# VectorE's exponential as five fp16 bit patterns that TensorE sums in PV, on three of sixteen key blocks per unit instead of two

## The chip, the cores and the metric

The kernel runs on one core of a Trainium2 chip. The metric is device microseconds of one execution, median of three. A core has TensorE (PE, matrix multiplication into PSUM), ScalarE (ACT, here the exponential), VectorE (DVE), GpSimd (POOL), SyncE (SP, which issues DMAs), and 16 DMA engines. Each engine runs its own instructions in the order in which they were written, and waits on semaphores for the others.

## What is computed

Two attention problems of sequence length 2048, width 512 and 32 heads of 16 channels are computed, and their outputs stand side by side. Problem A works in four segments of 512 tokens: causal attention inside a segment, mixed by a gate with a linear-attention memory of the earlier segments. Problem B is plain full attention over 2048 keys. Cut to what matters here:

```python
def _B_ref(x, wqkv, wo):
    q, k, v = split_heads(x @ wqkv)                  # (B, H, S, 16) each
    scores = jnp.einsum('bhqd,bhkd->bhqk', q, k) * Dh ** (-0.5)
    p = _softmax(scores, axis=-1)
    o = jnp.einsum('bhqk,bhkd->bhqd', p, v)
    return merge_heads(o) @ wo

# A, per segment s: o = g * (phi(q) M) / (phi(q) z + 1e-6) + (1 - g) * causal_softmax(q k^T) v
return jnp.concatenate([a, b], axis=-1)
```

The work that dominates is the exponential of B's scores: 32 heads by 2048 queries by 2048 keys.

## The kernel before, in words

**Units.** The work is cut into 64 units, 32 of A and 32 of B. A unit is a chunk of 512 queries (`ch`), a group of eight heads (`rt`, 0 to 3) and one half of that group (`e`), so four heads `j`. The `order` list (L369 to L375) takes A's first segment, and then B's pairs of units (`e` 0 and 1) in turn with A's pairs of the later segments, until A's are used up; the last chunk of B has none between.

**Banks and tiles.** The scores of one key block (128 keys) for one head and 512 queries fill one PSUM bank, 128 x 512 in fp32. A unit of B has 16 key blocks of 4 banks, 64 in all; a pair of A units has 20. The banks that ScalarE is to exponentiate are put in a row and closed into tiles of alternately 3 and 2 banks (`BANKS`, L44; `close`, L415). For each tile `t` the loop at L757 writes, in this order: chores that are due (`run_until`), the score matmuls of the tile into `s_ps` and ScalarE's exponential of it into `pT` in bf16 (`scores`, L646, L655), the PV matmuls of up to two key blocks whose exponentials are at least two tiles old (`pv`, L730, called with `t - LAG`), some chores (projections, memory updates, outputs), filler matmuls (`idle_work`, L571), one score matmul for VectorE (`vscores`, L676), and as much VectorE work as its time credit allows (`vfill`, L632).

**PE's shapes.** Score matmuls contract over 32 rows, and the four heads use four row groups of the array. PV matmuls have 32 output columns, and the four heads use four column groups; a key block's four PV matmuls make one group of four. Projections use the whole array. All go through the helper `mm` (L77), so the profile gives them line L80 and they are told apart by their tiles. `mm` also counts an assumed cost in `work`. `idle_work` compares it with 74% of the tile's time (`PESHARE`) and issues matmuls of a zero matrix into the running accumulator (`acc<-zeros`) when PE has less to do than that.

**VectorE's exponential before.** For every B unit but the first, key blocks 0 and 1 (`VQUADS = 2`) are left out of ScalarE's tiles. Their scores go through a PSUM bank called `v_ps`. `vscores` scales and shifts each bank into 16-bit integers (L689, tile `vx`, four of them to a key block), so that the integer read as fp16 is a first estimate of the exponential. The generator `vexp` (L593) then corrects it by a polynomial: three tensor_scalar operations (L596) and three tensor_tensor operations (L599) on 128 x 2048 elements, in tiles `vf`, `vv` and `vx`. The result enters `pvq` as one more key block for PV. These blocks are planned over the span of the unit ahead of their own (L399, L424 to L444), so they are there when their unit begins.

**What holds things back.** `pvq` is sorted by unit, and `pv` works on one unit at a time, `cur`. PSUM has eight banks: five for the two score tiles, three under the tag `misc` (L335), which the unit's accumulator `acc`, `v_ps` and the PSUM of every projection share. When a unit's last PV matmul is written, `unit_done` (L694) has VectorE transpose the accumulator out and normalise it in pieces (`vfin`). The exponentials `pT` have six tiles in all (`PBUFS`).

**The check on sums.** `sums_ok` (L304) looks at all softmax denominators against `SUMS` (L35); out of bounds, a slow exact version would run at the end.

Of the kernel before, what the change touches and what calls it, by code (L numbers as in the profile page):

```python
# [34 lines left out]
SUMS = {"a": (2.0 ** -8, 2.0 ** 31), "b": (2.0 ** 7, 2.0 ** 15.5)}  # L35
XSCALE = SCALE * 1.4426950408889634 * 1024

C0, C1, C3 = 0.4580543, 0.4656991, 0.0762947
# [3 lines left out]
VWAIT = 3  # L42
VQUADS = 2
# [6 lines left out]
def kernel(  # L50
# [87 lines left out]
    def load_w(pool, name):  # L138

        t = pool.tile([P, 4, 3 * D], BF16, name=f"w_{name}", tag=f"w_{name}")  # L140
        srcs = ([B_wqkv[:, i * D:(i + 1) * D] for i in range(3)] if name == "b" else [A_wq, A_wk, A_wv])

        def load(eng, i, lo=0, hi=D):
            eng.dma_start(out=t[:, :, i * D + lo:i * D + hi],
                          in_=srcs[i][:, lo:hi].rearrange("(cc p) n -> p cc n", p=P))
        return t, load
# [20 lines left out]
    def do_k(mp, w, xT, rt, dst):  # L167
        ps = mp.tile([P, W], F32, name="k_ps", tag="misc")
        for cc in range(4):
            mm(ps[:], w[:, cc, D + rt * P:D + (rt + 1) * P], xT[:, cc, :], start=(cc == 0), stop=(cc == 3))  # L170
            if cc == 3:
                vlater(0.69, lambda: pin(nc.vector.tensor_copy(dst, ps[:])))
            yield

    def do_q(mp, wk, w, xT, rt, dst, phi=None):

        ps = mp.tile([P, W], F32, name="q_ps", tag="misc")
        for cc in range(4):
            mm(ps[:], w[:, cc, rt * P:(rt + 1) * P], xT[:, cc, :], start=(cc == 0), stop=(cc == 3))
# [22 lines left out]
    def do_v(mp, w, xT, kb, dst):  # L202
        ps = mp.tile([P, W], F32, name="v_ps", tag="misc")
        for cc in range(4):
            mm(ps[:], xT[:, cc, kb * P:(kb + 1) * P], w[:, cc, 2 * D:3 * D], start=(cc == 0), stop=(cc == 3))
# [124 lines left out]
    with ExitStack() as ms:  # L330
# [6 lines left out]
        wA, ld = load_w(big, "a")  # L337
# [8 lines left out]
        wB, ld = load_w(big, "b")  # L346
# [32 lines left out]
        for name, ch, rt in order:  # L379
# [4 lines left out]
            if name == "a":  # L384
# [7 lines left out]
                spans.append([(name, ch, rt), banks, []])  # L392
            else:

                for u in us:
                    quads_left[u["id"]] = S // P
                    nv = VQUADS if nb else 0
                    if nb:
                        spans[-1][2].extend((u, kb) for kb in range(nv))  # L399
                    spans.append([(name, ch, rt) if u is u0 else None,  # L400
                                  [(j, [(u, kb, 0, 512, 0)]) for kb in range(nv, S // P) for j in q4], []])
                    nb += 1

        for i in range(1, len(spans)):
            key = spans[i][0]
            if key and key[0] == "a" and spans[i][2]:
                spans[i - 1][1] += spans[i][1]
                spans[i - 1][2] += spans[i][2]
                spans[i - 1].append((key, len(spans[i - 1][1]) - len(spans[i][1])))
                spans[i] = None  # L410
        first_tile, tiles = {}, []
        vq = deque()
        act = deque()

        def close(n, v=None):  # L415
            tiles.append(([act.popleft() for _ in range(n)], v))
        for sp in spans:
            if sp is None:
                continue
            starts = {0: sp[0]} if sp[0] else {}  # L420
            for key, at in sp[3:]:
                starts[at] = key
            for u, kb in sp[2]:
                vq.append((u, kb, set(q4)))  # L424
            nv, na, placed = sum(len(left) for *_, left in vq), len(sp[1]), 0
            for i, bank in enumerate(sp[1]):
                if i in starts:
                    first_tile[starts[i]] = len(tiles)
                act.append(bank)
                n = BANKS[len(tiles) % 2]  # L430
                if len(act) < n:
                    continue
                v = None
                if vq and placed < nv and (placed + 0.5) * na <= nv * (i + 1):
                    js = vq[0][2] - {j for j, _ in act}
                    if js:
                        j = min(js)
                        u, kb, left = vq[0]
                        left.discard(j)
                        if not left:  # L440
                            vq.popleft()
                        first_tile.setdefault(("v", u["ch"], u["rt"]), len(tiles))
                        v = (j, (u, kb, 0, 512, 0))
                        placed += 1  # L444
                close(n, v)
        assert not vq
        while act:
            close(min(BANKS[len(tiles) % 2], len(act)))
# [70 lines left out]
        def b_kv_chores():  # L519
            v_ones(VB, S // P)  # L520
            for rt in range(NRT):
                for ch in range(4):
                    d = first_tile[("b", 0, rt)] + 5 * ch
                    chore(min(d, first_tile.get(("v", 0, rt), NT)) if ch == 0 else d,
                          do_k(mp, wB, xTB[ch], rt, KB[:, rt, ch * W:(ch + 1) * W]))
            for sb in range(S // P):
                chore(first_tile[("b", 0, 0)] + 4 + 4 * sb // 3,
                      do_v(mp, wB, xTB[sb // 4], sb % 4, v_heads(VB, sb)[:, :, 0:DH]))


        vfin, vwork, credit = deque(), deque(), [0.0]
# [46 lines left out]
        pvq = []  # L578
# [12 lines left out]
        vx, live = {}, [0]  # L591

        def vexp(q, xq):  # L593

            def ts(o, i, s1, s2, op0, op1):
                pin(nc.vector.tensor_scalar(o, i, s1, s2, op0, op1))  # L596

            def tt(o, i0, i1, op):
                pin(nc.vector.tensor_tensor(o, i0, i1, op=op))  # L599
            yield 0.69  # L600
            assert live[0] < 3
            live[0] += 1
            f = wk.tile([P, 4, 512], F16, name="vf", tag="vf")
            v = wk.tile([P, 4, 512], F16, name="vv", tag="vv")
# [7 lines left out]
            yield 0.69  # L612
# [3 lines left out]
            pd = xq[:].bitcast(F16)  # L616
            u, kb = q
            pvq.append(dict(u=u, kb=kb, t=now[0], v=True, parts=[(pd, j, j, (u, kb, 0, 512, 0)) for j in q4]))
            pvq.sort(key=lambda q: q["u"]["id"])
# [12 lines left out]
        def vfill(us):  # L632
            credit[0] = min(credit[0] + us, 1.4)
            while vfin or vwork:
                wq = vfin or vwork
                if wq is vwork and live[0] == 3 and not wq[0][2]:
# [9 lines left out]
        def scores(t):  # L646
            banks, vb = tiles[t]
# [17 lines left out]
            for sl, (j, segs) in enumerate(banks):  # L665
                for seg in segs:
# [5 lines left out]
                    q["parts"].append((pT, sl, j, seg))  # L672
                    q["t"] = t
            pvq.sort(key=lambda q: q["u"]["id"])

        def vscores(t):  # L676

            vb = tiles[t][1]
            if vb is None:
                return  # L680
            vt = mp.tile([P, 512], F32, name="v_ps", tag="misc")
            score(vt[:], vb[0], vb[1], True)
            u, kb = vb[1][0:2]
            if (u["id"], kb) not in vx:
                while len(vwork) >= VWAIT:
                    vpiece(vwork)
                vx[u["id"], kb] = [wk.tile([P, 4, 512], U16, name="vx", tag="vx", bufs=VWAIT + 2), 0]
            x = vx[u["id"], kb]
            pin(nc.vector.tensor_scalar(x[0][:, vb[0], :], vt[:], XSCALE, 15360.0, ALU.mult, ALU.add))  # L689
            x[1] += 1  # L690
            if x[1] == 4:
                vpush(vwork, vexp((u, kb), x[0]))
# [37 lines left out]
        def pv(t, lim):  # L730
# [7 lines left out]
            for q in ready[0:lim]:  # L738
                pvq.remove(q)
                live[0] -= "v" in q  # L740
# [6 lines left out]
                for pT, sl, j, (_, kb, col, w, c0) in q["parts"]:  # L747
# [9 lines left out]
        for t in range(NT):  # L757
# [13 lines left out]
            idle_work(0.1 + 0.427 * len(tiles[t][0]))  # L771
            flush()
            vscores(t)
            vfill((0.08 + 0.427 * len(tiles[t][0])) * VSHARE - (0.69 if tiles[t][1] else 0.0))
# [5 lines left out]
        vdrain(vwork)  # L780
# [41 lines left out]
    def exact_problem(name):  # L822
        is_a = name == "a"
        with ExitStack() as es:
# [17 lines left out]
            w, ld = load_w(big, name)  # L842
# [119 lines left out]
```

## Time and profile before

| quantity | value |
|---|---|
| median of three runs | 1050.23 us |
| the three runs | 1049.83, 1050.23, 1059.84 us |
| span of the profiled execution, first to last instruction | 1055.6 us |
| own time of the profiled execution | taken as 1059.84 us, the only one of the three longer than the span |
| mean granted TensorE clock | 0.976 of full |
| ScalarE busy | 984.7 us |
| TensorE busy | 967.6 us |
| VectorE busy | 759.8 us |
| GpSimd busy | 169.9 us |

How to read it: the span starts at the first and ends at the last instruction, and the own time holds what lies around it too (4.2 us here). Busy is the time in which at least one instruction of an engine was running. Matmuls overlap one another, so their mean duration is longer than the distance from one to the next; the same holds for ScalarE's exponentials. A row of the groups gives busy time, the mean ns of one instruction, and the idle time of the engine just before them with the instruction that ended it. The waits list who stood idle for whom. The chain follows the work that ended last back to the start.

### The profile page before, as it was taken

The page shows a single profiled execution, that of the slowest core. Times are in us where ns is not written, and L with a number is a line of the kernel's source. Part 1 is how long each engine was busy: PE and PEld are TensorE (multiplying, and loading weights), DVE is VectorE, ACT ScalarE, POOL GpSimd, SP SyncE. Part 2 cuts the span into 40 slices and gives each one's busy share as a digit, 9 for nine tenths or more (in the row PEclk, how much of TensorE's full clock was granted, in tenths as well). Part 3 has the DMA queues.
Part 4 walks back from the last instruction along what each step waited for, and adds up shares of the span by engine and source line. Part 5 has one row for each costly group of instructions (what it writes and reads, how often), then busy time and mean ns, then how long its engine had stood idle before and what let it go on. Part 6 is the DMA issues. An engine that isn't in the chain of part 4 may idle for free.

```text
span 1055.6 us, 17191 instructions
## 1 busy us (share of the span) xinstructions
PE 967.6 (92%) x6822; PEld 277.2 (26%) x6822; DVE 759.8 (72%) x1108; ACT 984.7 (93%) x877; POOL 169.9 (16%) x335
## 2 busy tenths in 40 slices
PE   8899999998999989999998999999999999999996
PEld 2222222222222222222222222222222222222221
DVE  2668787866888677788876788858576787776654
ACT  3799999998999989999999899999999999999995
POOL 3721210403013030030302204021020300000000
PEclk8999999998999989999999899999999999999998
DMA  8400000001000000010000000000000000000000
GB/s 179 100 7 21 6 2 6 1 2 25 6 1 13 29 7 6 2 25 6 2 6 1 21 26 1 7 1 1 2 1 1 2 30 11 1 1 2 1 1 25
DMA packets 35642, 15.36 MB, mean 15 GB/s; under 512 B 27360, under 2 KB 35552, under 8 KB 35552
## 3 DMA queue, kind: packets, MB, share of 16 engines
q1 hardware_dynamic: 33776, 13.78, 5.5%
q8 instruction: 55, 0.90, 0.4%
q10 hardware_dynamic: 1776, 0.40, 0.2%
q14 instruction: 35, 0.29, 0.1%
HBM read 4.20 MB, written 4.19 MB: 8 GB/s over the span
## 4 chain that ended last, share of the span: by engine, by line
ACT 40%; PE 31%; issue 12%; DVE 11%; POOL 3%; DMA 1%; SPq 0%; ACTq 0%; DVEq 0%; POOLq 0%
ACT pT L655 39%; PE acc L80 14%; PE s_ps L80 8%; PE v_ps L80 5%; DVE vv L599 2%; DVE vx L689 2%; POOL pT L663 2%; PE q_ps L80 1%; PE k_ps L80 1%; DVE vx L599 1%; PE o_ps L80 1%; DVE vv L596 1%; ACT ex L194 1%; DVE vf L596 1%; DVE tT L253 1%
## 5 line engine op out<-in xcount | busy, mean ns | idle before, releaser
L655 ACT ACTIVATE pT<-s_ps 128x1536 bf16<-128x1536 f32 x848 | 973.5, 1314 | 57.7 <-PE s_ps L80 53.0
L80 PE MATMUL s_ps<-qB,KB 32*128 32x512 bf16 x1800 | 310.8, 384 | 35.0 <-ACT pT L655 30.5
L80 PE MATMUL acc<-zeros 128*128 128x512 bf16 x1053 | 321.6, 390 | 0.0
L689 DVE TENSOR_SCALAR vx<-v_ps 128x512 uint16<-128x512 f32 x248 | 169.1, 683 | 122.2 <-PE v_ps L80 65.7
L80 PEld LDWEIGHTS <-KB 32*128 32x128 bf16 x2048 | 99.6, 91 | 339.6 <-issue 326.7
L663 POOL TENSOR_SCALAR_AFFINE_SELECT pT<-pT 128x256 bf16<-128x256 bf16 (+2 forms) x242 | 111.0, 487 | 322.7 <-ACT pT L655 322.1
L80 PE MATMUL acc<-pT,VB 128*32 128x512 bf16 x1800 | 144.4, 385 | 1.2 <-DVE tT L253 1.2
L80 PEld LDWEIGHTS <-zeros 128*128 128x128 bf16 x1069 | 84.6, 99 | 147.2 <-issue 111.7
L253 DVE STREAM_TRANSPOSE tT<-acc 128x512 f32<-128x512 f32 x64 | 45.7, 714 | 94.1 <-PE acc L80 93.9
L80 PE MATMUL v_ps<-qB,KB 32*128 32x512 bf16 x248 | 95.5, 385 | 9.2 <-DVE aT L260 3.4
L596 DVE TENSOR_SCALAR vv<-vv 128x2048 f16<-128x2048 f16 x124 | 86.7, 699 | 2.2
L599 DVE TENSOR_TENSOR vv<-vf 128x2048 f16<-128x2048 f16 x62 | 76.2, 1229 | 1.9
L599 DVE TENSOR_TENSOR vx<-vx,vv 128x2048 int16<-128x2048 uint16 x62 | 76.0, 1226 | 1.2
L599 DVE TENSOR_TENSOR vv<-vv,vf 128x2048 f16<-128x2048 f16 x62 | 76.0, 1227 | 1.1
L80 PE MATMUL s_ps<-qA,kA 32*128 32x384 bf16 (+3 forms) x512 | 56.8, 313 | 9.9 <-ACT pT L655 7.8
L186 POOL TENSOR_SCALAR qB<-qc,par 128x512 bf16<-128x512 bf16 x32 | 26.0, 823 | 232.1 <-DVE qc L183 229.2
L80 PEld LDWEIGHTS <-VB 128*32 128x32 bf16 x2048 | 32.4, 94 | 73.9 <-issue 73.8
L596 DVE TENSOR_SCALAR vf<-vx 128x2048 uint16<-128x2048 uint16 x62 | 43.3, 699 | 1.5
L186 POOL TENSOR_SCALAR qA<-qc,par 128x512 bf16<-128x512 bf16 x32 | 25.7, 815 | 114.9 <-DVE qc L183 114.8
L80 PE MATMUL acc<-pT,vA 128*32 128x128 bf16 (+3 forms) x512 | 39.0, 332 | 5.6 <-POOL pT L663 3.2
L80 PEld LDWEIGHTS <-kA 32*128 32x128 bf16 x512 | 17.8, 92 | 63.1 <-issue 61.2
L80 PE MATMUL acc<-vx,VB 128*32 128x512 f16 x248 | 24.7, 386 | 4.6 <-DVE vx L599 3.9
(88 smaller groups left out, 510.8 us busy)
## 6 DMA issues: line engine op xcount, KB each, us to landing
out_dram<-osb SPq DMA_DIRECT2D x31, 128.0 KB, 1.7
w_b<-in_B_wqkv_dram SPq DMA_DIRECT2D x3, 512.0 KB, 6.0
phk<-phkT SPq DMA_TRANSPOSE x48, 2.3
w_a<-in_A_wv_dram SPq DMA_DIRECT2D x1, 512.0 KB, 7.0
wo_a<-in_A_wo_dram SPq DMA_DIRECT2D x1, 512.0 KB, 4.1
wo_b<-in_B_wo_dram SPq DMA_DIRECT2D x1, 512.0 KB, 5.0
w_a<-in_A_wk_dram SPq DMA_DIRECT2D x1, 384.0 KB, 7.5
w_a<-in_A_wq_dram SPq DMA_DIRECT2D x1, 384.0 KB, 8.2
```

The costliest lines, as they stand in the source:

```text
L80: return pin(nc.tensor.matmul(out, lhsT, rhs, **k))
L186: pin(nc.gpsimd.tensor_scalar(dst[:, e, :], qc[:], par[:, e:e + 1], 0.0, ALU.mult, ALU.add))
L194: pin(nc.scalar.activation(ex[:], src, ACT.Exp))
L253: vlater(0.72, lambda: pin(nc.vector.transpose(st["tT"][:, e].rearrange("p c d -> p (c d)"), acc)))
L596: pin(nc.vector.tensor_scalar(o, i, s1, s2, op0, op1))
L599: pin(nc.vector.tensor_tensor(o, i0, i1, op=op))
L655: pin(nc.scalar.activation(pT[:, 0:n, :], pt[:, 0:n, :], ACT.Exp, scale=SCALE))
L663: pin(nc.gpsimd.affine_select(out=blk, in_=blk, compare_op=ALU.is_ge, fill=0.0, base=0, pattern=[[0, len(sls)], [1, P]], channel_multiplie ...
L689: pin(nc.vector.tensor_scalar(x[0][:, vb[0], :], vt[:], XSCALE, 15360.0, ALU.mult, ALU.add))
```

## The change

VectorE's share goes from two to three key blocks of sixteen in each B unit but the first. Its polynomial is taken out. A block's exponential is now a sum of five fp16 numbers: the scaled scores as 16-bit integers plus one of five offsets (`LADDER`), each read as fp16. The first comes from the scaling itself; each of the other four is one tensor_scalar (add, then min with 32767) on 128 x 2048 elements into a tile of its own. PV takes each of the five as a key block of its own with the same weights, so TensorE's accumulation makes the sum, in the denominator (the ones column) as well.

The tiles of ScalarE are closed over the row of banks alone, and VectorE's scores follow a plan of their own (`vplan`): blocks 1 and 2 during the unit itself up to a cut, `VLEAD` = 12 banks early, and block 0 of the next unit from the cut to that unit's start. The cut lies at two thirds of the unit where a B unit follows directly, at 83% (`VEND`) elsewhere. One score matmul is written per tile, or two when the plan is over three tiles late. The 16-bit tiles share nine buffers (`VBUFS`); two of them hold B's key and value weights until those projections are done, so the weights are now three tiles instead of one. `scores` writes PV matmuls or VectorE steps first (`force`) when the `pT` tile six back still has PV matmuls unwritten. `VPOOL` is 0, so GpSimd makes no step. The bounds on B's sums become 2^9 and 2^15.

```diff
-C0, C1, C3 = 0.4580543, 0.4656991, 0.0762947
+LADDER = (12521, 12721, 12834, 13081, 13329)
...
-VWAIT = 3
-VQUADS = 2
+VBUFS = 9
+VQUADS = (3, 3)
+VEND = 0.83
+VLEAD = 12
+VPOOL = 0
...
-        wB, ld = load_w(big, "b")
+        wB, ld = load_w([(big, "wb0", 1)] + [(wk, "vx", VBUFS)] * 2, "b")
...
+                    nv = u["nv"] = VQUADS[nb % 2] if nb else 0
+                    quads_left[u["id"]] = S // P + nv * (len(LADDER) - 1)
...
+        def plan(u, kbs, lo, hi):
+            for i in range(4 * len(kbs)):
+                t = tile_of[int(lo - VLEAD + (i + 0.5) * (hi - lo) / (4 * len(kbs)))]
+                first_tile.setdefault(("v", u["ch"], u["rt"]), t)
+                vplan.append((t, u, kbs[i // 4]))
+        for u, nxt in zip(bs, bs[1:] + [None]):
+            n = max(u["nv"], 2)
+            cut = u["lo"] + (u["hi"] - u["lo"]) * ((n - 1) / n if nxt and nxt["lo"] == u["hi"] else VEND)
+            plan(u, range(1, u["nv"]), u["lo"], cut)
+            if nxt:
+                plan(nxt, range(1), cut, nxt["lo"])
...
-            ts(f[:].bitcast(U16), xq[:], 0x3FF, 0x3C00, ALU.bitwise_and, ALU.bitwise_or)
-            yield 1.22
-            tt(v[:], f[:], f[:], ALU.mult)
-            yield 0.69
-            ts(v[:], v[:], C3, C1 - 1.0, ALU.mult, ALU.add)
-            yield 1.22
-            tt(v[:], v[:], f[:], ALU.mult)
-            yield 0.69
-            ts(v[:], v[:], C0, 1024.0, ALU.add, ALU.mult)
-            yield 1.22
-            tt(xq[:].bitcast(I16), xq[:], v[:], ALU.add)
...
+        def vexp(q, buf, x):
+
+            for i, off in enumerate(LADDER[1:]):
+                yield 0.0 if i < VPOOL else 0.70
+                f = vtile()
+                if i < VPOOL:
+                    pin(nc.gpsimd.tensor_scalar(f[:], x[:], 1.0, float(off - LADDER[0]), ALU.mult, ALU.add))
+                else:
+                    pin(nc.vector.tensor_scalar(f[:], x[:], float(off - LADDER[0]), 32767.0, ALU.add, ALU.min))
+                vready(q, [1], f, 2 * (i < VPOOL))
+                vdone(buf)
...
         def scores(t):
-            banks, vb = tiles[t]
+            banks = tiles[t]
+            while apend.get(t - PBUFS):
+                force()
...
         def vscores(t):
 
-            vb = tiles[t][1]
-            if vb is None:
+            n = 0
+            while vplan and vplan[0][0] <= t and n < 1 + (vplan[0][0] < t - 3):
+                _, u, kb = vplan[0]
+                if (u["id"], kb) not in vx:
+                    if vlive[0] > VBUFS - 2:
+                        break
+                    vx[u["id"], kb] = [vtile(), set(q4)]
...
+                vt = mp.tile([P, 512], F32, name="v_ps", tag="misc")
+                score(vt[:], j, (u, kb, 0, 512, 0), True)
+                pin(nc.vector.tensor_scalar(x[:, j, :], vt[:], XSCALE, float(LADDER[0]), ALU.mult, ALU.add))
+                n += 1
+                if not left:
+                    buf = [len(LADDER)]
+                    vready((u, kb), buf, x)
+                    vpush(vwork, vexp((u, kb), buf, x))
+            return n
+
+        def force():
+            forced[0] += 1
+            if pv(NT, 1):
                 return
...
+            if vwork and vlive[0] < VBUFS:
+                vpiece(vwork)
+                return
+            assert step_chore()
...
-            vfill((0.08 + 0.427 * len(tiles[t][0])) * VSHARE - (0.69 if tiles[t][1] else 0.0))
+            vfill((0.08 + 0.427 * len(tiles[t])) * VSHARE - 0.69 * vscores(t))
```

More of the change, by code (lines that the diff above doesn't have):

```diff
@@ L411 @@
[L411 to L428, printed above, removed]
-                act.append(bank)
[L430 to L445, printed above, removed]
@@ L446 @@
-        assert not vq
-        while act:
-            close(min(BANKS[len(tiles) % 2], len(act)))
+        first_tile, tiles, act, tile_of = {}, [], deque(), []
+        for key, banks, u in spans:
+            if key:
+                first_tile[key] = len(tiles)
+            if u:
+                u["lo"] = len(tile_of)
+            for bank in banks:
+                act.append(bank)
+                tile_of.append(len(tiles))
+                if len(act) == BANKS[len(tiles) % 2]:
+                    tiles.append([act.popleft() for _ in range(len(act))])
+            if u:
+                u["hi"] = len(tile_of)
@@ L520, in b_kv_chores, with counted @@
             v_ones(VB, S // P)
+            left = {"k": S // P, "v": S // P}
+            def counted(which, g):
+                yield from g
+                left[which] -= 1
+                vlive[0] -= left[which] == 0
             for rt in range(NRT):
@@ L671, in scores @@
                         pvq.append(q)
[L672 removed]
+                    q["parts"].append((pT, sl, j, seg, t))
                     q["t"] = t
+                    apend[t] = apend.get(t, 0) + 1
             pvq.sort(key=lambda q: q["u"]["id"])
         def vscores(t):
[L678 to L692 removed]
+            n = 0
[5 more added lines that the diff above has]
+                    vx[u["id"], kb] = [vtile(), set(q4)]
+                vplan.popleft()
+                x, left = vx[u["id"], kb]
+                j = min(left, key=lambda j: (j in {j for j, _ in tiles[t]}, j))
+                left.discard(j)
+                vt = mp.tile([P, 512], F32, name="v_ps", tag="misc")
[10 more added lines that the diff above has]
+            if pv(NT, 1):
+                return
+            if vwork and vlive[0] < VBUFS:
+                vpiece(vwork)
+                return
+            assert step_chore()
         def unit_done(u):
```

84 lines of the change are left out of this document (39 added, 45 removed).

## The prediction, on record before the result

> **What bounds the kernel now.** The page's head comes first: busy time by engine, then the slices of the two busiest.
>
> ```profile
> span 1055.6 us, 17191 instructions
> PE 967.6 (92%) x6822; PEld 277.2 (26%) x6822; DVE 759.8 (72%) x1108; ACT 984.7 (93%) x877; POOL 169.9 (16%) x335
> ACT  3799999998999989999999899999999999999995
> ```
>
> ScalarE is busy for 984.7 of 1055.6 us and TensorE for 967.6, so either could be the bound. ScalarE's slices say 9 nearly everywhere but at the start. The groups tell which of the two does work that has to be done:
>
> ```profile
> L655 ACT ACTIVATE pT<-s_ps 128x1536 bf16<-128x1536 f32 x848 | 973.5, 1314 | 57.7 <-PE s_ps L80 53.0
> ...
> L80 PE MATMUL acc<-zeros 128*128 128x512 bf16 x1053 | 321.6, 390 | 0.0
> L689 DVE TENSOR_SCALAR vx<-v_ps 128x512 uint16<-128x512 f32 x248 | 169.1, 683 | 122.2 <-PE v_ps L80 65.7
> L80 PE MATMUL v_ps<-qB,KB 32*128 32x512 bf16 x248 | 95.5, 385 | 9.2 <-DVE aT L260 3.4
> L596 DVE TENSOR_SCALAR vv<-vv 128x2048 f16<-128x2048 f16 x124 | 86.7, 699 | 2.2
> L599 DVE TENSOR_TENSOR vv<-vf 128x2048 f16<-128x2048 f16 x62 | 76.2, 1229 | 1.9
> L599 DVE TENSOR_TENSOR vx<-vx,vv 128x2048 int16<-128x2048 uint16 x62 | 76.0, 1226 | 1.2
> L599 DVE TENSOR_TENSOR vv<-vv,vf 128x2048 f16<-128x2048 f16 x62 | 76.0, 1227 | 1.1
> L596 DVE TENSOR_SCALAR vf<-vx 128x2048 uint16<-128x2048 uint16 x62 | 43.3, 699 | 1.5
> ```
>
> 848 exponentials make up 973.5 us of ScalarE, each of real scores. Of TensorE's time 321.6 us are matmuls of zeros that the program adds where its own estimate finds TensorE under 74%; the work that counts is 967.6 - 321.6 = 646 us. TensorE is full because it is filled. ScalarE stands idle 57.7 us ahead of its exponentials, 53.0 of them for scores from TensorE. The waits show the two sides of that hand-over and what TensorE itself waits for:
>
> ```profile
> ACT pT L655 <- PE s_ps L80: 53.0, 61, 8.0
> PE s_ps L80 <- ACT pT L655: 38.3, 115, 1.0
> PE v_ps L80 <- DVE aT L260: 4.2, 3, 2.0
> PE acc L80 <- DVE vx L599: 3.9, 7, 1.0
> ```
>
> TensorE waits 38.3 us for ScalarE to free a score tile, in 115 short waits: the normal state of a full ScalarE. Its waits for VectorE are small (4.2 and 3.9 us). So ScalarE sets the end, behind a start-up in which it has nothing to do. How much slack is behind it differs by stage; first the zeros alone, then all engines, in the same five windows (columns: window, length, busy and count of PE and PEld, in the second table also of DVE, ACT and POOL, then clock, DMA share, GB/s):
>
> ```profile
> 60.00:100.00 40.00, 3.56 (x11) 0.83 (x11) 0.00 (x0) 1.00 0.05 14
> 100.00:150.00 50.00, 8.29 (x26) 2.22 (x26) 0.00 (x0) 1.00 0.02 6
> 150.00:400.00 250.00, 74.15 (x235) 19.77 (x235) 0.00 (x0) 0.97 0.04 10
> 400.00:700.00 300.00, 95.83 (x302) 25.30 (x303) 0.00 (x0) 0.98 0.04 9
> 700.00:1040.00 340.00, 138.80 (x477) 34.26 (x475) 0.00 (x0) 0.99 0.01 4
> ```
>
> ```profile
> 60.00:100.00 40.00, 37.20 (x263) 10.27 (x262) 30.01 (x47) 37.92 (x35) 6.47 (x14) 1.00 0.05 14
> 100.00:150.00 50.00, 45.86 (x333) 13.22 (x331) 39.01 (x61) 47.34 (x44) 10.47 (x19) 1.00 0.02 6
> 150.00:400.00 250.00, 229.62 (x1628) 65.18 (x1629) 192.03 (x280) 236.54 (x212) 44.45 (x79) 0.97 0.04 10
> 400.00:700.00 300.00, 275.31 (x1971) 78.48 (x1967) 229.01 (x343) 288.30 (x260) 48.83 (x87) 0.98 0.04 9
> 700.00:1040.00 340.00, 320.39 (x2250) 91.61 (x2249) 236.49 (x317) 333.96 (x295) 25.51 (x51) 0.99 0.01 4
> ```
>
> Without zeros TensorE has 84%, 75%, 62%, 60% and 53% of the five windows to do, and ScalarE runs at 95%, 95%, 95%, 96% and 98%. VectorE is at 70 to 78%. The least slack is from 60 to 150 us, where B's projections are made.
>
> **The change part by part.** *ScalarE (removed).* One key block less per B unit, 31 units of 4 banks: 124 banks, 2120 to 1996. 848 tiles in 973.5 us are 424 pairs of 5 banks, 2.296 us a pair. 124 / 5 = 24.8 pairs, 56.9 us. The 3-bank and 2-bank tiles alternate as before, so the mean holds. This lies on the path at full price.
>
> *VectorE (exchanged).* A block cost 4 x 0.683 (L689) + 3 x 0.699 (L596) + 3 x 1.227 (L599) = 8.51 us, and 62 blocks 528 us. Now it costs 4 x 0.683 plus four steps on 128 x 2048. No row shows a 16-bit integer add. The nearest are L596 on uint16 and fp16, 0.699 each, one input and the same size, and above it L599, 1.226, with two inputs, whose result is also an integer sum. I take 0.699, since L596 has the same kind of instruction and shape and keeps its time over both 16-bit types. 93 x (2.73 + 2.80) = 514 us, so VectorE goes from 759.8 to about 746 us. At 1.226 the 372 steps add 372 x 0.527 = 196 us. [...]
>
> *TensorE, PV (added).* 93 blocks of five groups instead of 62 of one, and 31 fewer from ScalarE: 512 groups of four in B become 419 + 465 = 884, 372 more. What a group costs is read from the starts in the timeline (start, length, instruction, count):
>
> ```profile
> 602.84 0.61 PE L80 MATMUL acc<-pT,VB 128*32 128x512 bf16 x8
> ...
> 603.39 0.39 PE L80 MATMUL o_ps<-wo_b,OT_b 128*128 128x512 bf16 x1
> ...
> 603.71 0.39 PE L80 MATMUL s_ps<-qB,KB 32*128 32x512 bf16 x2
> ```
>
> ```profile
> 608.85 0.40 PE L80 MATMUL acc<-vx,VB 128*32 128x512 f16 x4
> 609.07 0.39 PE L80 MATMUL acc<-pT,VB 128*32 128x512 bf16 x4
> ```
>
> Two groups (x8) take 0.55 us to the next start, one matmul of another shape 0.32, and a group followed by a group of the same shape 0.22 (608.85 to 609.07). So 0.22 in company and 0.32 alone, and fp16 costs no more than bf16: 372 x 0.22 to 0.32 = 82 to 119 us. I take 0.24, 90 us, since `pv` writes up to two groups in a row. [...]
>
> *TensorE, scores.* 49 tiles fewer at about 0.32 us each, 16 us off; 124 single score matmuls more at up to 0.385 (row v_ps), less where one starts with the tile's own scores as at 607.47 below: 10 to 48 us. Together about nothing to 30 us.
>
> *Zeros (they give way).* The program counts a PV group at 0.256 us and takes that from the filler, and ScalarE's shorter time takes 0.74 x 57 = 42 us more: 372 x 0.256 + 42 = 137 us at 0.213 are up to 640 of 1053 zeros. Some are kept, since a surplus over 0.25 us is forgotten; I expect 400 to 560 left. At 321.6 / 1053 = 0.305 us a zero they give back 150 to 200 us, more than PV takes. This is the cover for PV's 90 us: where zeros stand now. Per pair of B units and the pair of A units beside it (20 + 104 banks, 57 us) 24 groups are 5.3 us, 9 points. With the shorter span the five windows' real share goes to about 90%, 90%, 76%, 74% and 68%: full only in the first two.
>
> *What does not stay covered.* With ScalarE's share against TensorE's real share in the table, going from 53% to 84% costs 3.5 points of ScalarE, and between 62% and 84% nothing. A step of 14 points thus costs between 0 and 1.5 points, 0 to 15 us over 980; I take 6. The early windows, 60 to 150 us at 90%, add 3 us, an estimate with 0 and 8 as ends. And each of 124 more scores needs one of the three shared PSUM banks:
>
> ```profile
> 607.47 0.37 PE L80 MATMUL v_ps<-qB,KB 32*128 32x512 bf16 x1 [0.52 <-DVE osb L319]
> ...
> 608.17 1.45 ACT L655 ACTIVATE pT<-s_ps 128x1536 bf16<-128x1536 f32 x1 [0.27 <-PE s_ps L80]
> ```
>
> Here a `v_ps` matmul waits 0.52 us for VectorE's `osb`, and ScalarE behind it 0.27. The row of v_ps has 9.2 us of idle for 248; 124 more at that rate, 0.037, are 5 us, of which perhaps one or two reach ScalarE. At most each would wait a full eviction, 0.683.
>
> *At nothing.* The weights as three tiles come by the same loads in the same order on SP's queue. A VectorE step now waits for one of nine buffers, so for PV of an older block, and evictions stand behind it on VectorE; a block's five tiles are through PV within the unit, and the steps are written only when the count has room, so I put this wait at nothing, with the late blocks below as its price if the cover is gone. The start-up is unchanged, as is the tail, which begins when the last scores are done; VectorE's last block is planned to end at 83% of its unit.
>
> *Sum.* The profiled execution is taken to be the run of 1059.84, the only one longer than its span (1055.6 and 4.2 around it): 1059.8 - 56.9 + 6 + 3 + 1.5 = 1013. The median, 1050.2, is 9.6 lower, so against it 1003.6, say 1003 us.
>
> **The rivals.** *The gaps shrink too.* Part of ScalarE's idle time comes behind waits of TensorE for VectorE's transposes `aT` of A's units (4.2 us in 3 waits, the longest 2.0, above). VectorE's steps get shorter, 0.70 at most instead of 1.23, so evictions behind them come sooner. For it: VectorE is in the way in those waits. Against: the transposes are themselves the wait. Of the 57.7 us some 24 are start-up (ScalarE's first two slices, 26.4 us each, read 3 and 7), which leaves 34; half of these less gives 993 - 17 = 976, a third 982; with some of the costs above, 985.
>
> *TensorE becomes the bound for most of the run.* For it: 92% busy already, in order, and zeros are written without knowledge of a backlog. With PV alone in each group (119 us), scores at 30, and only 150 us of zeros given back, TensorE goes from 967.6 to 967 us, in a run that is to be 57 us shorter. With its present 88 us of idle, 4 around the span and 10 off to the median that is 1049; 38.3 of the idle are waits for ScalarE, and with half of these gone it is 1030. Against: the zeros counted above.
>
> *A step on VectorE costs 1.226.* VectorE then has 943 us. At 95% from 25 us on, with tail and surroundings, 943 / 0.95 + 25 + 9 + 4 is 1031; with the 78% to 90% that an engine coupled to two others reaches it is over 1080. I put it at 1060. Against: both rows of L596.
>
> *Slower: TensorE stands behind VectorE for a PSUM bank.* The place is the `v_ps` matmul in `vscores`. All later scores are queued behind it on TensorE, and ScalarE waits for those. `acc` holds one of three banks, two when units change over, and then two scores in one tile, or one and a projection, leave none. 372 waits at 0.25 us are 93 instead of 9, and 993 + 84 gives 1077. It decides from 0.18 us per score ((57 + 9) / 372), and it ends at 0.683. For it: the row at 607.47. Against: 9.2 us in 248.
>
> *VectorE's blocks come late.* Before, they were computed one unit ahead; now in the unit. If the last step comes after the last scores, PV holds the unit open, and with six `pT` tiles ScalarE stops. A block of steps is 2.8 us, and 31 units at 1.5 us are 46: 1040. Against: the plan leaves a third of a unit, 8 us, behind block 2.
>
> **How the numbers follow.** Forecast 1003 (own range 992 to 1020) 0.52; smaller gaps, 985, 0.14; TensorE bound, 1030, 0.15; dear step, 1060, 0.04; PSUM wait, 1077, 0.09; late blocks, 1040, 0.06. About 1% is what a measurement of this kernel can tell from no change, 1039.7 to 1060.7. Faster takes the first two, most of the third (0.13) and half of the last (0.03): 0.82. Same takes the rest of both and half of the dear step: 0.07. Slower takes the PSUM wait and the other half: 0.11. The range 982 to 1045 leaves out the low half of the second case and the slow ones, under 0.2.
>
> **What would show it.** ScalarE: about 799 exponentials and 917 us. VectorE: 372 steps of 0.70 and 746 us. PV from `vx`: 1860 matmuls. Zeros: 400 to 560. TensorE near 92% busy all the same, and ScalarE's idle for `s_ps` 50 to 65 us. Wrong if steps take over 1 us, if TensorE's waits for VectorE pass 40 us, or if ScalarE's share falls under 90%.

## The result, and the profile after

The changed kernel takes 1015.68 us in the median of four runs (1006.52 to 1027.83); the kernel before, measured beside it, took 1050.03. The ratio is 0.9614, 95% interval 0.9529 to 0.9699: faster by 3.9%, or 40 us, where 47 were forecast. The profiled execution is the longest of the four, 1027.83 us with a span of 1026.1; the ratio leaves it out as disturbed, and below it serves for counts and places, not for the total. The runs also list spans beside times: 1.7 us lie around the span, not 4.2, so the profiled execution of before was not the 1059.84 run. In the prediction's sum this cancels, since the distance to the median shrinks by as much.

The head of the page after, with ScalarE's slices and the granted clock (tenths of full):

```profile
span 1026.1 us, 18868 instructions
PE 923.2 (90%) x7597; PEld 254.6 (25%) x7721; DVE 726.6 (71%) x1232; ACT 934.4 (91%) x828; POOL 162.2 (16%) x335
ACT  3799976789999999999999979999999999999984
PEclk8999975689999999999999999999999999999988
```

ScalarE and TensorE are still the busiest, but there is a dip from the sixth to the ninth slice, 128 to 231 us, in ScalarE's row and the clock's at once. The groups that answer to those of before (busy, mean ns | idle before and its releaser):

```profile
L648 ACT ACTIVATE pT<-s_ps 128x1536 bf16<-128x1536 f32 (+1 forms) x799 | 923.9, 1313 | 78.1 <-PE s_ps L83 65.1
L685 DVE TENSOR_SCALAR vx<-v_ps 128x512 uint16<-128x512 f32 x372 | 254.1, 684 | 176.5 <-PE s_ps L83 117.9
L83 PE MATMUL s_ps<-qB,KB 32*128 32x512 bf16 x1676 | 319.7, 394 | 33.3 <-ACT pT L648 24.9
L608 DVE TENSOR_SCALAR vx<-vx 128x2048 uint16<-128x2048 uint16 x372 | 243.8, 692 | 1.2
...
L83 PE MATMUL acc<-vx,VB 128*32 128x512 f16 x1860 | 170.4, 396 | 4.1 <-DVE vx L685 1.7
L83 PE MATMUL v_ps<-qB,KB 32*128 32x512 bf16 x372 | 146.9, 395 | 19.2 <-issue 5.6
...
L83 PE MATMUL acc<-pT,VB 128*32 128x512 bf16 x1676 | 155.3, 398 | 0.0
L83 PE MATMUL acc<-zeros 128*128 128x512 bf16 x401 | 132.4, 398 | 6.9 <-issue 6.8
...
L83 PEld LDWEIGHTS <-zeros 128*128 128x128 bf16 x480 | 38.8, 99 | 90.5 <-issue 78.3
```

The counts are as worked out: 799 exponentials, 372 VectorE steps at 0.692 us, 1860 PV matmuls from `vx`. Of zeros there are 464, not the 401 of the matmul row: this trace lacks some matmul records, but each zero matmul has a weight load of its own, and the last row has 480 loads, 16 of them (`PREWARM`) from before the loop. In the kernel before, no zero is missing (1053). So TensorE's 90% is a little too low, and zeros are counted by their weight loads from here on. ScalarE's row fell from 973.5 to 923.9, 50 of the 57 us. Its idle time before exponentials rose from 57.7 to 78.1 (an exponential that begins late also loses its overlap with the one before, 0.20 us in the mean of those that do not; in a kernel with fewer late ones, further down, the row is at 917.1). VectorE is at 726.6, some 20 us under the forecast. TensorE's waits for VectorE add up to 28 us, as before. The same windows as before, all engines, show where ScalarE is short:

```profile
60.00:100.00 40.00, 36.61 (x272) 10.27 (x273) 24.75 (x42) 38.63 (x36) 5.99 (x13) 1.00 0.05 14
100.00:150.00 50.00, 44.34 (x337) 11.44 (x339) 33.84 (x58) 42.59 (x37) 8.20 (x17) 0.91 0.02 6
150.00:400.00 250.00, 228.85 (x1809) 59.23 (x1839) 179.90 (x304) 223.07 (x197) 38.59 (x77) 0.89 0.04 10
400.00:700.00 300.00, 271.90 (x2358) 78.16 (x2397) 228.95 (x397) 287.93 (x258) 51.23 (x100) 0.99 0.03 9
700.00:1010.00 310.00, 284.58 (x2451) 77.31 (x2489) 225.81 (x371) 300.85 (x266) 23.17 (x43) 0.98 0.02 5
```

Its shares are 97%, 85%, 89%, 96% and 97%: the loss is between 100 and 400 us, with a clock of 0.91 and 0.89. Ten microseconds at a time:

```profile
140.00:150.00 10.00, 7.87 (x48) 1.75 (x48) 6.87 (x13) 6.97 (x6) 1.73 (x2) 0.73 0.00 0
150.00:160.00 10.00, 9.67 (x42) 1.57 (x42) 4.97 (x10) 6.92 (x6) 1.48 (x2) 0.50 0.01 2
160.00:170.00 10.00, 8.87 (x43) 1.52 (x43) 4.97 (x8) 5.97 (x5) 0.00 (x0) 0.50 0.00 0
170.00:180.00 10.00, 9.66 (x58) 1.56 (x57) 5.83 (x11) 6.40 (x5) 0.00 (x0) 0.50 0.00 1
180.00:190.00 10.00, 9.53 (x56) 1.57 (x53) 4.53 (x8) 6.42 (x6) 0.00 (x0) 0.50 0.01 2
190.00:200.00 10.00, 9.47 (x72) 1.84 (x71) 6.52 (x11) 7.74 (x8) 0.00 (x0) 0.71 0.06 13
...
220.00:230.00 10.00, 8.97 (x79) 2.50 (x78) 8.12 (x16) 9.68 (x9) 0.00 (x0) 1.00 0.01 2
```

The clock is granted at half from 144.6 to 195.8 us. TensorE is some 94% busy there (the mean from 150 to 190) but gets through 42 to 58 matmuls in 10 us instead of 79, and ScalarE is fed for 60 to 70%. VectorE is idle about half the time there. In this stretch it is TensorE that is late.

The four runs stand in the order of their clocks: 1006.5 us at a mean clock of 0.983, 1010.8 at 0.979, 1020.6 at 0.965, 1027.8 at 0.955, some 7.6 us for each hundredth of clock. The time at half clock in the profiled execution, called cold time, is 93 us against 50 before. In the trace's clock record every cold stretch but the last, which the end cuts off, is a whole number of 3.41 us: 1, 2, 3, 4 or 15 of them.

### The profile page after: what moved, and what is told of

Read it like the earlier page. It is cut to its first block, busy times and chain, and to the rows that moved or that the text cites. A ratio compares the mean times of both kernels' runs of the same rounds, so it can differ in the third digit from the quotient of the medians.

```text
span 1026.1 us, 18868 instructions
## 1 busy us (share of the span) xinstructions
PE 923.2 (90%) x7597; PEld 254.6 (25%) x7721; DVE 726.6 (71%) x1232; ACT 934.4 (91%) x828; POOL 162.2 (16%) x335
## 4 chain that ended last, share of the span: by engine, by line
ACT 42%; PE 32%; issue 12%; DVE 9%; POOL 2%; DMA 1%; SPq 0%; ACTq 0%; DVEq 0%
ACT pT L648 41%; PE acc L83 14%; PE s_ps L83 8%; PE v_ps L83 6%; DVE vx L685 3%; PE k_ps L83 2%; PE q_ps L83 1%; DVE vx L608 1%; PE o_ps L83 1%; DVE tT L256 1%; ACT ex L197 1%; POOL pT L656 1%; DMA w_a<-in_A_wv_dram 1%; DVE qc L186 1%; SPq L159 0%
## 5 line engine op out<-in xcount | busy, mean ns | idle before, releaser
L648 ACT ACTIVATE pT<-s_ps 128x1536 bf16<-128x1536 f32 (+1 forms) x799 | 923.9, 1313 | 78.1 <-PE s_ps L83 65.1
L685 DVE TENSOR_SCALAR vx<-v_ps 128x512 uint16<-128x512 f32 x372 | 254.1, 684 | 176.5 <-PE s_ps L83 117.9
L83 PE MATMUL s_ps<-qB,KB 32*128 32x512 bf16 x1676 | 319.7, 394 | 33.3 <-ACT pT L648 24.9
L608 DVE TENSOR_SCALAR vx<-vx 128x2048 uint16<-128x2048 uint16 x372 | 243.8, 692 | 1.2
L83 PE MATMUL acc<-vx,VB 128*32 128x512 f16 x1860 | 170.4, 396 | 4.1 <-DVE vx L685 1.7
L83 PE MATMUL v_ps<-qB,KB 32*128 32x512 bf16 x372 | 146.9, 395 | 19.2 <-issue 5.6
L83 PE MATMUL acc<-zeros 128*128 128x512 bf16 x401 | 132.4, 398 | 6.9 <-issue 6.8
L83 PEld LDWEIGHTS <-VB 128*32 128x32 bf16 x3536 | 56.8, 95 | 141.6 <-issue 140.9
L83 PEld LDWEIGHTS <-zeros 128*128 128x128 bf16 x480 | 38.8, 99 | 90.5 <-issue 78.3
L186 DVE CAST qc<-q_ps 128x512 bf16<-128x512 f32 x32 | 21.9, 683 | 16.2 <-PE q_ps L83 14.6
L322 DVE CAST osb<-o_ps 128x512 bf16<-128x512 f32 x28 | 19.2, 684 | 7.7 <-PE o_ps L83 7.3
L83 PE MATMUL v_ps<-w_a,xT_a 128*128 128x512 bf16 x60 | 21.1, 426 | 3.1 <-DMA w_a<-in_A_wv_dram 1.6
```

The lines of the kernel that those rows point to most:

```text
L83: return pin(nc.tensor.matmul(out, lhsT, rhs, **k))
L322: vlater(0.69, lambda: pin(nc.vector.tensor_copy(osb[:], ps[:])))
L608: pin(nc.vector.tensor_scalar(f[:], x[:], float(off - LADDER[0]), 32767.0, ALU.add, ALU.min))
L648: pin(nc.scalar.activation(pT[:, 0:n, :], pt[:, 0:n, :], ACT.Exp, scale=SCALE))
L685: pin(nc.vector.tensor_scalar(x[:, j, :], vt[:], XSCALE, float(LADDER[0]), ALU.mult, ALU.add))
```

## The experiments

Three theories: **load** (TensorE has too much real work, and scores come late at full clock too), **clock** (with few zeros left TensorE falls to half clock and stays there), **hand-over** (score matmuls wait for VectorE to empty PSUM banks). Where runs taken at different times are compared, each goes by its ratio to the kernel before as measured beside it, times 1050 us; a ratio of 0.001 is one microsecond. The changed kernel's own runs differ in clock, and so its ratio is the least certain (0.9529 to 0.9699). Where it matters, single runs at the same clock are compared as well.

**More zeros.**

```diff
-PESHARE = 0.74
+PESHARE = 0.80
```

> The changed kernel with the filler's target raised from 74% to 80% (PESHARE). Three theories on why it stands at about 1010 us and not at the 993 that ScalarE's shorter row alone would give, with runs from 1006 to 1028. Clock theory: with 401 zero matmuls left of 1053, TensorE passes windows of little full-array work, its clock is granted at half for whole windows (82 us of cold time in the profile after, against 34 before), and while it is at half the real work alone fills it, so it stays there; more zeros cut the cold time to under 35 us, the time falls to 995 to 1005 and the runs lie closer together. Load theory: TensorE has too much real work (about 75 to 90% of the windows), scores come late at full clock too; some 250 more zeros of 0.3 us push it further, the time rises to 1015 to 1035. Hand-over theory: the score matmuls wait for VectorE to empty shared PSUM banks; zeros change nothing, 1005 to 1015.

1017.79 us (six runs, 1014.06 to 1019.62), ratio 0.9676, 0.9643 to 0.9709. The clock rose to 0.988 and the runs moved together, as the clock theory has it, but the time did not fall, as the load theory has it. It has 673 zeros by their weight loads against 464. ScalarE still waits for TensorE with the clock near full:

```profile
L648 ACT ACTIVATE pT<-s_ps 128x1536 bf16<-128x1536 f32 (+1 forms) x799 | 924.8, 1257 | 66.3 <-PE s_ps L83 52.6
```

Filler buys clock and pays with load, and here the two come out even.

**No zeros.**

```diff
-PESHARE = 0.74
+PESHARE = 0.0
```

> The changed kernel without any filler (PESHARE 0): 401 zero matmuls fewer, 132 us of TensorE. Clock theory: the clock stays at half for long stretches, real work of over 700 us at full clock needs up to twice as long there, and the time rises to 1050 or more, with a mean granted clock under 0.9. Load theory: TensorE has more room and the time falls to 995 to 1005. Hand-over theory: unchanged, 1005 to 1015.

1168.7 us, ratio 1.1112, 1.1048 to 1.1177, clock 0.69. Its clock by slices:

```profile
PEclk8989956558775965895577995555557596555566
```

The load theory by itself falls: over 132 us less work on TensorE made it 157 us slower.

**The kernel before with as few zeros.**

```diff
-PESHARE = 0.74
+PESHARE = 0.58
```

> The kernel before, with the filler's target lowered from 74% to 58%, so that 418 zero matmuls of 1053 are left, about as many as in the changed kernel; nothing else. It has 635 x 0.305 = 194 us less on TensorE. Load theory: not slower, 1040 to 1050, as TensorE has more room. Clock theory: the granted clock falls from 0.986 to under 0.97 and the time rises to 1058 or more: fewer zeros are a cost by themselves.

1162.8 us in the median (1125.04 to 1180.97), clock 0.805 in the shortest run, against 1053.2 and 0.973 to 0.988 for the kernel before, measured beside it. Its runs lie too far apart for a ratio with an interval; the shortest is 72 us slower than the median of before. The prediction called zeros the cover under which PV costs nothing. They are not free room: with PV not yet there to replace them, taking 635 of them away costs 72 us or more, though it is some 194 us less work for TensorE.

**Two blocks instead of three.**

```diff
-VQUADS = (3, 3)
+VQUADS = (2, 2)
```

> The changed kernel with two key blocks of sixteen instead of three, so ScalarE's row of exponentials is that of the kernel before (848 tiles, 973 us) and all else, the patterns, the plan in the unit and the buffers, is as in the change. If the gain is ScalarE's shorter row alone: 1045 to 1055, no difference from before. If the patterns and the plan cost time of their own (TensorE's 186 more PV groups): 1055 to 1065. If they thin out the stalls: 1035 to 1045.

1039.57 us, ratio 0.9891, 0.9843 to 0.9939, with ScalarE's row as before (848 exponentials, 970.9 us). So all of the change but the third block (patterns, plan and buffers, not told apart here) is worth 11 us (6 to 16 by the interval) with no exponential saved, the third of the three cases expected. The page has VectorE at 576.8 us against 759.8, and the row of exponentials an idle time of 43.7 us against 57.7:

```profile
PE 918.9 (89%) x7399; PEld 275.4 (27%) x7525; DVE 576.8 (56%) x984; ACT 980.6 (95%) x877; POOL 171.5 (17%) x335
L648 ACT ACTIVATE pT<-s_ps 128x1536 bf16<-128x1536 f32 x848 | 970.9, 1369 | 43.7 <-PE s_ps L83 30.9
```

The third block then brings 1050 x (0.9891 - 0.9614) = 29 us of its 57.

**PV of one pattern.**

```diff
-quads_left[u["id"]] = S // P + nv * (len(LADDER) - 1)
+quads_left[u["id"]] = S // P
...
-                vready(q, [1], f, 2 * (i < VPOOL))
+                vlive[0] -= 1
```

> The changed kernel in which VectorE makes all five patterns but PV takes the first alone; the other four are made and not summed, so the output lacks most of VectorE's three blocks. TensorE has 372 PV groups fewer (82 to 119 us), and the filler puts zeros in their place (by its own count 372 x 0.256 / 0.213, some 400 more). Clock theory: the clock holds, 992 to 1003. Load theory: TensorE's real work falls to under that of before, 992 to 1003 as well, with ScalarE's idle for scores under 55 us. Hand-over theory: the score matmuls still wait for VectorE, 1003 to 1015. If PV is covered, as the prediction said, within 6 us of the changed kernel.

994.01 us, ratio 0.9451, 0.9411 to 0.9491, at a clock of 0.978 to 0.983. The changed kernel at 0.983 took 1006.5: at one clock, PV's 372 groups cost 12 us more than what takes their place (386 more zeros, by their weight loads), and 17 by the ratios. PV was not covered. The edit also frees PV from waiting for VectorE's last four patterns, but those waits stood at only 1.3 us (TensorE's `acc` for VectorE's L608).

**No steps on VectorE.**

```diff
-                    vready((u, kb), buf, x)
-                    vpush(vwork, vexp((u, kb), buf, x))
+                    for _ in LADDER:
+                        vready((u, kb), buf, x)
```

> The changed kernel in which PV takes VectorE's first pattern five times over and VectorE makes none of the other four, so the output has a wrong weight on its three blocks. TensorE's matmuls are all there; VectorE does 372 steps, 244 us, less. Load theory and clock theory (TensorE is what ScalarE waits for): no gain, 1003 to 1015. Hand-over theory (TensorE waits on VectorE's queue): VectorE falls to about 480 us busy, score matmuls find their banks free, 990 to 1000.

1000.34 us, ratio 0.9491, 0.9448 to 0.9534, between the two ranges expected: 244 us less on VectorE are worth 13 us though TensorE does all its matmuls; at one clock it is 7 us (999.1 at 0.984 against 1006.5 at 0.983). ScalarE's idle row names TensorE all the same:

```profile
L648 ACT ACTIVATE pT<-s_ps 128x1536 bf16<-128x1536 f32 (+1 forms) x799 | 921.7, 1317 | 53.1 <-PE s_ps L83 40.2
```

So VectorE has a part in it, which its 71% do not show.

**The row-group conflict.** The timeline after showed something that the prediction had not looked at. A `v_ps` matmul starts together with the tile's scores, and the next group comes 0.53 us later:

```profile
645.84 0.11 PEld L83 LDWEIGHTS <-KB 32*128 32x128 bf16 x3 [0.42 <-issue]
645.85 0.38 PE L83 MATMUL v_ps<-qB,KB 32*128 32x512 bf16 x1
645.85 0.59 PE L83 MATMUL s_ps<-qB,KB 32*128 32x512 bf16 x2
...
646.38 0.39 PE L83 MATMUL acc<-zeros 128*128 128x512 bf16 x1
```

Scores alone take 0.32. The two scores last 0.59 us together; without a conflict they last 0.39 (the pair further down). `vscores` picks a head that the tile just written does not use, but what runs beside it is the next tile, and that begins with the very heads left over. Two matmuls on the same 32 rows run one behind the other here, 0.21 us more. All three weight loads are recorded within 0.11 us, beside the running `v_ps`; it is a score matmul that starts late, 0.22 us after the other.

```diff
-                j = min(left, key=lambda j: (j in {j for j, _ in tiles[t]}, j))
+                nxt = {j for j, _ in tiles[t + 1]} if t + 1 < NT else set()
+                j = min(left, key=lambda j: (j in nxt, j))
```

> The changed kernel with one line different: VectorE's next score matmul takes a head whose row group of the array the next tile's scores leave free, where there is one, instead of one that the tile just written leaves free. In the trace after, a v_ps matmul and the tile's scores behind it take 0.53 us to the next start, against 0.32 for scores alone: the two share a row group and run one behind the other, 0.21 us each time, 372 times, 78 us of TensorE. Load theory: with most of that gone TensorE's real work is as light as with one PV pattern (372 groups fewer, 994 us), so 995 to 1003. Clock theory alone: the matmuls are the same in number, so the cold time and the time stay, 1005 to 1015. If the conflict is not what costs 0.21: no change either, and the 0.53 stays in the trace.

1000.94 us (six runs, 1000.07 to 1001.95), ratio 0.9489, 0.9458 to 0.9519. Of the 2-bank score groups behind a `v_ps`, the median from its start to the next group is 0.33 us instead of 0.53. A 3-bank tile leaves only one head free, and behind it the median stays at 0.59. By the ratios this is 13 us without a matmul taken away. At one clock it is less: 1000.1 us against 1006.5 at 0.983, and 1001.4 to 1002.0 at 0.980 against 1010.8 at 0.979. So 6 to 9 us come of the lighter load itself. The rest goes with the clock, which is steadier here (0.980 to 0.984), or lies inside the ratios' intervals.

**The same, and waiting for a free row.**

```diff
+                if not left - nxt and vplan[0][0] >= t - 2:
+                    break
                 vplan.popleft()
```

> As free_row, and a score matmul for VectorE that has no head with a free row group is put off by a tile or two, until it is over two tiles late. More of the 372 conflicts go: load theory 992 to 1001, and at least as fast as free_row; clock theory alone 1005 to 1015; if the later scores make VectorE's blocks late, slower than free_row by 2 to 10 us.

991.65 us (six runs, 990.68 to 992.93), ratio 0.9401, 0.9370 to 0.9431: 22 us under the changed kernel by the ratios and 14 at one clock (992.9 at 0.984 against 1006.5 at 0.983), and the fastest version that computes all. Its timeline has the pair at 0.32 us, and its page TensorE at 86% (this trace lacks as many matmul records as the one after):

```profile
646.56 0.39 PE L83 MATMUL v_ps<-qB,KB 32*128 32x512 bf16 x1
646.56 0.39 PE L83 MATMUL s_ps<-qB,KB 32*128 32x512 bf16 x2
...
646.88 0.61 PE L83 MATMUL acc<-pT,VB 128*32 128x512 bf16 x8
```

```profile
PE 852.3 (86%) x7594; PEld 260.0 (26%) x7719; DVE 724.9 (73%) x1232; ACT 926.9 (94%) x828; POOL 165.8 (17%) x335
L648 ACT ACTIVATE pT<-s_ps 128x1536 bf16<-128x1536 f32 (+1 forms) x799 | 917.1, 1347 | 49.9 <-PE s_ps L83 46.2
L83 PE MATMUL s_ps<-qB,KB 32*128 32x512 bf16 x1676 | 266.6, 384 | 59.6 <-ACT pT L648 47.5
```

ScalarE's idle row is down from 78.1 to 49.9, its busy time at 917.1, the number that was forecast. The row of B's scores takes 266.6 us of TensorE instead of 319.7. With nearly the same zeros (462) the clock is 0.984 to 0.989 instead of 0.955 to 0.983; why it holds better was not tried.

**Two blocks with the free row.** `VQUADS = (2, 2)` on top of the last.

> free_row_wait with two key blocks per unit instead of three. It tells what the third block is worth once the row-group conflict is gone; with the conflict it was worth 1039.6 against some 1010, 30 of the 57 us of ScalarE's row. Load theory: with TensorE lighter the third block is worth nearly its price, so this stands 45 to 57 us over free_row_wait, 1036 to 1048, with less than 5 us to gain from the free row itself at two blocks. If the third block still loses half of its worth elsewhere: 1015 to 1030.

1044.0 us (nine runs), ratio 0.9913, 0.9881 to 0.9946. Without the conflict the third block brings 1050 x (0.9913 - 0.9401) = 54 of its 57 us; with it, 29. At two blocks the free row is worth nothing (0.9913 against 0.9891, intervals overlapping), as the load theory has it: TensorE has room there.

**No steps with the free row.** The edit of `no_steps` on top of `free_row_wait`.

> free_row_wait with PV taking VectorE's first pattern five times and VectorE making none of the other four (the output has a wrong weight on three blocks). In the changed kernel that was worth 9 to 15 us. Hand-over theory: VectorE's queue costs that by itself, so again 6 to 15 us under free_row_wait, 977 to 986. Load theory: it was worth something because TensorE was full and took VectorE's delays at full price; with TensorE lighter under 4 us are left, 987 to 993.

983.92 us, ratio 0.9332, 0.9285 to 0.9379: 7 us under `free_row_wait`, also at one clock (984.9 at 0.986 against 991.7), inside what the hand-over theory gave and over the load theory's 4. The edit makes PV a little cheaper too: its two rows together keep TensorE busy for 273.7 us against 277.9, which could account for 4 of the 7. So a part of VectorE's cost is its own, but a small one, and which of its waits it is was not separated further.

**Three and four blocks in turn.** `VQUADS = (3, 4)` on top of `free_row_wait`.

> free_row_wait with three and four key blocks in turn. ScalarE loses 4 banks in 15 or 16 units, 60 to 64 banks, 28 us. TensorE gets about 190 more PV groups, 42 to 60 us, VectorE some 86 us, to about 815. Load theory: TensorE is near full again, so of the 28 us a half to nothing comes through, 978 to 993. If ScalarE's row alone decides: 964. If VectorE's blocks come late: over 993.

1218.69 us, ratio 1.1568, 1.1511 to 1.1626. The third case, late blocks, and far beyond its bound. ScalarE saves 28 us and waits 300:

```profile
ACT pT L648 <- PE s_ps L83: 296.8, 88, 11.4
...
PE acc L83 <- DVE vx L608: 71.8, 195, 2.2
...
PE v_ps L83 <- DVE vx L688: 15.4, 55, 1.5
```

ScalarE's waits are up to 11.4 us long, and TensorE waits in PV for a VectorE step 195 times; VectorE itself is at 67%. This fits the prediction's rival of late blocks, in which the last steps come after the unit's last scores and the unit stays open. At three blocks PV's wait for a step stands at 1.3 us, so the margin ends between three and three and a half. Whether the plan or the nine buffers make the blocks late was not tried.

**More zeros with the free row.** `PESHARE = 0.78` on top of `free_row_wait`.

> free_row_wait with the filler's target at 78%. Its cold time is 34 us of 991, much of it at the start and the end, so the clock has little to give: clock theory 986 to 990, load theory 992 to 999 (134 more zeros at up to 0.3 us are 40 us of TensorE). In the changed kernel six points more of filler brought the clock to 0.988 and no time.

994.56 us (990.05 to 995.98), ratio 0.9439, 0.9401 to 0.9477, no better than without (0.9401). The clock is 0.984 to 0.992.

## Why the prediction was right, and where its sum was not

*Bound by ScalarE:* held, as far as TensorE lets it. 124 banks off its row are worth 54 us where TensorE has room, against 56.9 worked out.

*VectorE's step at 0.699:* held, 0.692. The rivals of a dear step and of 0.25 us per PSUM wait fell (of the shares that gave the dear step its 1060, 78% is VectorE's in the table of before, 39.01 of 50 us; 90% was an estimate that no run shows); idle before `v_ps` is 19.2 us for 372, 0.052 each, against the 0.18 from which it would have decided. The cost of up to 7 us that `no_steps_free` shows for VectorE's steps was in no term.

*Gaps that shrink:* taken as a rival at 0.14, true in part. Patterns and plan give 11 us at two blocks. The sum left this gain out.

*What does not stay covered:* the step that was mis-sized. It had 10.5 us for TensorE's crowding and the new scores; by the ratios it is 57 + 11 - 40 = 28, if the 11 us hold at three blocks too. The rival that TensorE becomes the bound, put at 0.15, came true in this part. The shares of ScalarE in the five windows of before were read as a price list for load, and in that kernel load between 62% and 84% cost nothing. The new work came in at other places. The edits of `pv_one` (17 us by the ratios, 12 at one clock), `free_row_wait` (22 and 14) and `no_steps` (13 and 7) each bring a part of the 28 back, and the parts overlap, so they cannot be added. The largest comes from the scores, which the prediction put at nothing to 30 us of TensorE and counted as covered. In conflict at 0.21 each, 372 are up to 78 us of TensorE, 26 of them new; the 53 us by which the row of B's scores falls without most conflicts is what was measured. The conflict stood in the timeline of before as well, in the very place that the prediction showed for `v_ps`: the three scores last 0.58 us instead of 0.39, and the next group begins 0.52 us after the `v_ps` instead of 0.32:

```profile
607.47 0.37 PE L80 MATMUL v_ps<-qB,KB 32*128 32x512 bf16 x1 [0.52 <-DVE osb L319]
...
607.48 0.58 PE L80 MATMUL s_ps<-qB,KB 32*128 32x512 bf16 x3
...
607.99 0.61 PE L80 MATMUL o_ps<-wo_a,OT_a 128*128 128x512 bf16 x2
```

With two blocks TensorE has room for it, as `two_blocks_free` shows; with three the room is gone.

*Zeros give way:* the count was right (464), the meaning was not. Zeros were room here only as far as real work came in their place: with 635 of them taken away and nothing put there, `before_few_zeros` lost 72 us or more. In the profiled execution the clock went to half and stayed there for 51 us, with TensorE some 94% busy, nearly all of it real work (8 of the 244 matmuls on record there are zeros). This goes with the spread of 21 us between the runs. It is shown by the kernels with fewer zeros that fewer zeros lowered the clock (to 0.805 or less and to 0.66 to 0.69) and cost time; that the clock makes the difference between the four runs rests on their order alone. What begins a stretch was not tried. The one at 144.6 us follows 1.64 us in which TensorE waits for VectorE's `kA`.

The two errors, 11 us of gain and 18 of cost not counted, partly cancel. That is luck: the forecast of 1003 lies 0.6% under the 1009.5 that the ratio gives, inside its own range of 992 to 1020.

## What to carry to other kernels

When work is moved to an engine that looks full of filler, cost it by the place where it is issued, next to which shapes, and not by the mean share of the window. Here matmuls were free beside one another only where the ones issued next to each other really were on separate row groups (0.32 us against 0.53 to the next group); look at what follows in the queue, not at what went before. Filler that keeps a clock up can be part of the load, as here (209 more zeros brought the clock to 0.988 and no time): vary it both ways before calling it slack.

## What the runs showed of the hardware that was not expected

In the profiled execution of the changed kernel half clock held for 51.2 us while TensorE was busy for 48.3 of them (94%), and in the kernel without zeros the row of the clock reads 5 in all six slices from 698 to 873 us. In the kernel before, going from 1053 zero matmuls to 418 took the mean clock from 0.973 to 0.988 down to 0.805 or less; in the changed kernel, with 372 more PV groups, about the same number (464) still gave 0.955 to 0.983, and none at all gave 0.66 to 0.69.
